# Gated linear attention and a dense block: one score product per 128-token chunk instead of seven levels of halving

## The chip, the cores and the metric

The kernel runs on one core of one Trainium2 chip. The metric is the device time of one execution in microseconds (us). The engines are PE (TensorE: matrix products and transposes), DVE (VectorE), ACT (ScalarE), POOL (GpSimd) and SP (SyncE, which here issues all transfers). Each engine works through its own queue in order.

## The reference

A recurrence over the tokens feeds a dense block.

```python
B, H, S, D = 4, 8, 768, 48          # q, k, v: randn * 0.1; alpha: uniform in 0.8 .. 1.0
for t in range(S):
    state = alpha[:, :, t, :, None] * state + einsum('bhd,bhe->bhde', k[:, :, t], v[:, :, t])
    y[:, :, t] = einsum('bhd,bhde->bhe', q[:, :, t], state)
x = y.transpose(0, 2, 1, 3).reshape(B * S, H * D)      # 3072 x 384
h = x @ w_in                                           # 384 x 2048
out = (h - tanh(h)) @ w_out                            # 2048 x 384
```

The weights come as float64 and everything is computed in fp32.

## The kernel before, in words

The 3072 tokens are worked in 12 units of 256 tokens, two chunks of 128 (c) each, three units to a batch entry. Two heads share the 128 partitions, 64 rows each, of which 48 hold features; g counts these four pairs, hh the head in a pair.

`gla(u)` is a unit's recurrence. It transposes alpha, k and q on PE (tiles an, kn, qn through tp, L185), so that features lie on the partitions. Then it goes through seven levels of halving (L204 to L236). At level l the block of 2 << l tokens has its left half (s) and its right half (t); the decay between them is a product from the middle to t (`pre`) times one from s to the middle (`suf`). At each level DVE multiplies q and k with these into W (L209, L213), PE makes 16 products of 128 rows by 64 columns (sc, L220), DVE copies the valid ones into `scores` under a mask (L225), and POOL extends suf and pre (L234, L235). The term s = t is made apart: qk and dv on POOL, dot on DVE. For each chunk PE then adds the old state's part (L246) and the scores' part (L249) into y; DVE adds dv, PE transposes x back, ACT stores xT. kT times suf is transposed (ks), multiplied with v (up, L269) and added to the decayed state by POOL and DVE (L278, L279).

`moe(u)` is the dense part. For each of 8 steps, `first(s)` makes h (L292: 6 products of 256 columns) and from it g = h - tanh(h), by a polynomial for small h: four operations on ACT (L301 to L304) and six on DVE (L305 to L310). `second(s)` adds g's product with w_out (L317: 4 products of 384 columns) to o0 and o1, two steps behind `first`. At the end ACT copies o to ob and SP writes it.

`weights()` loads w_in and w_out in 28 tiles and turns each from float64 into fp32 with six operations on DVE, two on ACT and one on POOL (L117 to L135); the tiles `raw` come from a pool of two buffers.

The order in which work is handed to the scheduler is a sorted list of numbered steps:

```python
MOE, GLA, EARLY = FS + 1, 1 + LEVELS + 2 * CU, 5.0
    order += [(u * MOE + i, 1, "moe", u) for i in range(MOE)]
    at = (u - 1) * MOE - EARLY
    order += [(at + i * MOE / GLA, 0, "gla", u) for i in range(GLA)]
```

So unit u's recurrence is spread over the dense part of the unit before it, and starts five steps early. The scheduler then fixes one order for each engine.

Of the kernel before, what the change touches and what calls it, by code (L numbers as in the profile page):

```python
# [8 lines left out]
FP32 = mybir.dt.float32  # L9
# [15 lines left out]
ZA = C4 ** 0.5  # L25
ZB = C3 / (2.0 * ZA)
ZK = C2 - ZB * ZB


@with_exitstack  # L30
def kernel(
# [14 lines left out]
    G = CU * NP  # L46
# [14 lines left out]
    consts = ctx.enter_context(tc.tile_pool(name="consts", bufs=1))  # L61
    two = ctx.enter_context(tc.tile_pool(name="two", bufs=2))
    three = ctx.enter_context(tc.tile_pool(name="three", bufs=3))
    ps_sc = ctx.enter_context(tc.tile_pool(name="ps_sc", bufs=2, space=PSUM))
    ps_tp = ctx.enter_context(tc.tile_pool(name="ps_tp", bufs=1, space=PSUM))
    ps_y = ctx.enter_context(tc.tile_pool(name="ps_y", bufs=1, space=PSUM))
    ps_h = ctx.enter_context(tc.tile_pool(name="ps_h", bufs=2, space=PSUM))
    ps_o = ctx.enter_context(tc.tile_pool(name="ps_o", bufs=1, space=PSUM))

    V, A, T, GP = nc.vector, nc.scalar, nc.tensor, nc.gpsimd  # L70
# [4 lines left out]
    V.memset(z_bias, ZB)  # L75
    m_bias = consts.tile([P, 1], FP32, name="m_bias")
# [4 lines left out]
    mask = consts.tile([P, LEVELS, P // 2], FP32, name="mask")  # L81
    GP.memset(mask, 1.0)
    for l in range(LEVELS):
        L = 1 << l
        m = mask[:, l, :].rearrange("p (n j) -> p n j", j=L)
        n = P // (2 * L)
        GP.affine_select(out=m, in_=m, compare_op=ALU.is_ge, fill=0.0, base=0,
                         pattern=[[-2 * L, n], [0, L]], channel_multiplier=1)
        GP.affine_select(out=m, in_=m, compare_op=ALU.is_ge, fill=0.0, base=L - 1,
                         pattern=[[2 * L, n], [0, L]], channel_multiplier=-1)  # L90
# [3 lines left out]
    nat = [[consts.tile([P, CU, H, HP], FP32, name=f"{n}{i}") for n in ("an", "kn", "qn")]  # L94
           for i in range(2)]
    for i in range(2):
        for t in nat[i]:
            GP.memset(t[:, :, :, D:], 0.0)
    scores = [consts.tile([P, 2, G, P], FP32, name=f"scores{i}") for i in range(2)]
    for t in scores:  # L100
        V.memset(t, 0.0)
    states = [consts.tile([P, NP, 2 * D], FP32, name=f"state{i}") for i in range(2)]
    for t in states:
        GP.memset(t, 0.0)
# [4 lines left out]
    def load_w(dst, src):  # L109
        """A part of a weight matrix, of up to 512 columns: from float64 rounded to fp32, with  # L110
        what fp32 has no normal number for as 0 or infinite."""
        if moe_w_in.dtype == FP32:
            nc.sync.dma_start(out=dst, in_=src)
            return
        n = dst.shape[-1]
        raw = two.tile([P, 512], I64, name="raw")
        nc.sync.dma_start(out=raw[:, 0:n], in_=src)  # L117
        words = raw.bitcast(I32).rearrange("p (n w) -> p n w", w=2)
        lo, hi = words[:, 0:n, 0].bitcast(mybir.dt.uint32), words[:, 0:n, 1]
        e = two.tile([P, 512], I32, name="e", tag="u")[:, 0:n]  # L120
        m = two.tile([P, 512], I32, name="m", tag="z")[:, 0:n]
        low = two.tile([P, 512], FP32, name="low", tag="t")[:, 0:n]
        man = two.tile([P, 512], FP32, name="man", tag="w")[:, 0:n]
        V.tensor_scalar(out=e, in0=hi, scalar1=20, scalar2=0x7FF,  # L124
                        op0=ALU.logical_shift_right, op1=ALU.bitwise_and)
        V.tensor_scalar(out=e, in0=e, scalar1=896, scalar2=1151, op0=ALU.max, op1=ALU.min)
        V.tensor_scalar(out=e, in0=e, scalar1=23, scalar2=0x3FFFFFFF,  # L127
                        op0=ALU.logical_shift_left, op1=ALU.bitwise_and)
        V.scalar_tensor_tensor(out=e, in0=hi, scalar=-0x40000000, in1=e,  # L129
                               op0=ALU.bitwise_and, op1=ALU.bitwise_or)  # L130
        V.tensor_single_scalar(out=m, in_=hi, scalar=0xFFFFF, op=ALU.bitwise_and)  # L131
        A.activation(man, m, AF.Copy, bias=1.0, scale=2.0 ** -20)
        A.activation(low, lo, AF.Copy, scale=2.0 ** -52)
        GP.tensor_add(man, man, low)
        V.tensor_mul(dst, man, e.bitcast(FP32))  # L135

    def weights():
        """In the order in which the first unit needs them."""
        w = 512
        for i in range(d_ff // w):  # L140
            for j in range(KT):
                load_w(w_in[:, j, i * w:(i + 1) * w], w_in_r[:, j, i * w:(i + 1) * w])
            yield
            for f in range(i * w // P, (i + 1) * w // P):
                load_w(w_out[:, f, :], w_out_r[:, f, :])
            yield

    loaded = {}

    def load(u):  # L150
        b, i = divmod(u, UPB)
        vt = three.tile([P, CU, H, D], FP32, name="vt")
        for c in range(CU):
            t0 = i * TU + c * P

            def rows(x):
                return x[b, :, t0:t0 + P, :].rearrange("h p d -> p h d")
            for t, x in zip(nat[u % 2], (alpha, k, q)):
                nc.sync.dma_start(out=t[:, c, :, 0:D], in_=rows(x))
            nc.sync.dma_start(out=vt[:, c], in_=rows(v))  # L160
        loaded[u] = vt

    xT = {}

    def gla(u):
# [4 lines left out]
        b, i = divmod(u, UPB)  # L170
        an, kn, qn = nat[u % 2]
        vt = loaded.pop(u)
        P_ = scores[u % 2]

        def unit(name, pool=two):
            return pool.tile([P, CU, NP, P], FP32, name=name)

# [4 lines left out]
        def flip(dst, src, copy):  # L182
            tp = ps_tp.tile([P, NP, P], FP32, name="tp")
            for g in range(NP):
                T.transpose(tp[:, g, :], src[:, 2 * g:2 * g + 2, :], ident)  # L185
# [193 lines left out]
```

## Time and profile before

| | |
|---|---|
| three runs | 1138.49, 1139.68, 1145.95 us (median 1139.68) |
| span of the profiled execution | 1140.3 us; its own time stands as this span |
| PE busy | 1045.0 us (92%) |
| PE weight loads (PEld) busy | 845.6 us (74%) |
| DVE busy | 805.0 us (71%) |
| ACT busy | 320.6 us (28%) |
| POOL busy | 342.8 us (30%) |
| mean granted PE clock | 0.909 of full speed |

A span is the time from the first to the last instruction. Busy times overlap between engines and add up to more than the span. Mean durations of PE's instructions overlap too, since matmuls are pipelined; the distance between starts says what one costs. In the rows, L220 is line 220 of the kernel, `sc<-W` is the output and the inputs, `64*128 64x64` are the shapes of the operands, and `x32` the number of instructions that a row merges. An idle time in brackets names what ended it.

### The profile page before, as it was taken

The page shows a single profiled execution, that of the slowest core. Times are in us where ns is not written, and L with a number is a line of the kernel's source. Part 1 is how long each engine was busy: PE and PEld are TensorE (multiplying, and loading weights), DVE is VectorE, ACT ScalarE, POOL GpSimd, SP SyncE. Part 2 cuts the span into 40 slices and gives each one's busy share as a digit, 9 for nine tenths or more (in the row PEclk, how much of TensorE's full clock was granted, in tenths as well). Part 3 has the DMA queues.
Part 4 walks back from the last instruction along what each step waited for, and adds up shares of the span by engine and source line. Part 5 has one row for each costly group of instructions (what it writes and reads, how often), then busy time and mean ns, then how long its engine had stood idle before and what let it go on. Part 6 is the DMA issues. An engine that isn't in the chain of part 4 may idle for free.

```text
span 1140.3 us, 14741 instructions
## 1 busy us (share of the span) xinstructions
PE 1045.0 (92%) x5752; PEld 845.6 (74%) x5752; DVE 805.0 (71%) x1212; ACT 320.6 (28%) x569; POOL 342.8 (30%) x293
## 2 busy tenths in 40 slices
PE   3765648999999999999999999999999999999988
PEld 2764548877877878778777788778787788777765
DVE  6688896584684677776774777685775676776766
ACT  2012330321421331421511431521502322413433
POOL 6454443043042044043132043143132152141000
PEclk9999755887998899989988999998979999989999
DMA  9433620110110020110200110200200000000000
GB/s 175 81 91 97 150 73 1 27 30 14 27 31 14 1 56 15 29 28 15 56 1 15 35 23 14 50 8 14 56 1 15 1 1 15 1 1 15 1 14 14
DMA packets 107396, 37.11 MB, mean 33 GB/s; under 512 B 100672, under 2 KB 103744, under 8 KB 107328
## 3 DMA queue, kind: packets, MB, share of 16 engines
q1 hardware_dynamic: 107328, 36.19, 14.1%
q8 instruction: 45, 0.74, 0.3%
q14 instruction: 23, 0.19, 0.1%
HBM read 31.46 MB, written 4.72 MB: 32 GB/s over the span
## 4 chain that ended last, share of the span: by engine, by line
PE 79%; DVE 15%; POOL 2%; issue 2%; ACT 1%; DMA 0%; SPq 0%; POOLq 0%; DVEq 0%
PE sc L220 24%; PE h L292 24%; PE o L317 20%; PE y L249 4%; DVE scores L225 3%; PE tp L185 2%; PE y L246 2%; PE up L269 2%; DVE e L129 1%; DVE W L209 1%; DVE z L307 1%; DVE e L127 1%; PE tp L265 1%; DVE m L131 1%; DVE e L124 1%
## 5 line engine op out<-in xcount | busy, mean ns | idle before, releaser
L220 PEld LDWEIGHTS sc<-W 64*128 64x128 f32 x2688 | 324.9, 217 | 92.7 <-issue 68.7
L220 PE MATMUL sc<-W 64*128 64x64 f32 x2688 | 338.1, 305 | 53.6 <-DVE W L213 41.0
L292 PE MATMUL h<-xT,w_in 128*128 128x256 f32 x1152 | 325.1, 426 | 5.1 <-DVE g L310 3.8
L317 PE MATMUL o<-w_out,g 128*128 128x384 f32 x768 | 278.7, 504 | 0.2 <-DVE g L310 0.2
L292 PEld LDWEIGHTS h<-xT,w_in 128*128 128x128 f32 x1152 | 231.7, 213 | 46.0 <-issue 4.8
L225 DVE COPY_PREDICATED scores<-mask,sc 128x512 f32<-128x512 int32 x168 | 147.8, 882 | 117.4 <-PE sc L220 115.1
L317 PEld LDWEIGHTS o<-w_out,g 128*128 128x128 f32 x768 | 147.5, 198 | 84.0 <-issue 7.7
L301 ACT ACTIVATE sq<-h 128x512 f32<-128x512 f32 x96 | 57.4, 598 | 440.9 <-PE h L292 437.1
L235 POOL TENSOR_TENSOR pre<-pre 128x512 f32<-128x512 f32 x84 | 118.3, 1409 | 115.5 <-DVE W L209 112.3
L234 POOL TENSOR_TENSOR suf<-suf,pre 128x512 f32<-128x512 f32 x72 | 100.3, 1393 | 140.3 <-DVE W L213 137.5
L305 DVE TENSOR_TENSOR w<-h,sq 128x512 f32<-128x512 f32 x96 | 66.2, 690 | 93.1 <-ACT th L302 92.4
L209 DVE TENSOR_TENSOR W<-qT,pre 128x512 f32<-128x512 f32 x84 | 60.1, 716 | 24.9 <-POOL pre L235 14.9
L310 DVE COPY_PREDICATED g<-large,h 128x512 f32<-128x512 int32 x96 | 70.6, 736 | 3.3
L309 DVE SCALAR_TENSOR_TENSOR g<-z,w 128x512 f32<-128x512 f32 x96 | 70.8, 737 | 1.8
L307 DVE SCALAR_TENSOR_TENSOR z<-z,sq 128x512 f32<-128x512 f32 x96 | 70.2, 731 | 0.0
L303 ACT ACTIVATE z<-sq,z_bias 128x512 f32<-128x512 f32 x96 | 69.6, 725 | 0.0
L304 ACT ACTIVATE large<-sq,m_bias 128x512 f32<-128x512 f32 x96 | 69.3, 722 | 0.0
L308 DVE SCALAR_TENSOR_TENSOR z<-z,sq 128x512 f32<-128x512 f32 x96 | 67.7, 705 | 1.9
L306 DVE TENSOR_TENSOR h<-h,th 128x512 f32<-128x512 f32 x96 | 66.7, 695 | 0.0
L213 DVE TENSOR_TENSOR W<-kT,suf 128x512 f32<-128x512 f32 x72 | 56.4, 784 | 14.2 <-POOL suf L234 14.2
L278 POOL TENSOR_TENSOR state<-state,pre 64x192 f32<-64x192 f32 x32 | 23.1, 722 | 139.3 <-DVE state L279 69.8
L249 PE MATMUL y<-vt,scores 128*128 128x48 f32 x384 | 53.2, 291 | 4.7 <-DVE scores L225 4.7
(60 smaller groups left out, 737.1 us busy)
## 6 DMA issues: line engine op xcount, KB each, us to landing
raw<-in_moe_w_in_dram SPq DMA_DIRECT2D x12, 512.0 KB, 3.9
raw<-in_moe_w_out_dram SPq DMA_DIRECT2D x16, 384.0 KB, 3.1
an<-in_alpha_dram SPq DMA_DIRECT2D x24, 192.0 KB, 3.3
kn<-in_k_dram SPq DMA_DIRECT2D x24, 192.0 KB, 3.5
qn<-in_q_dram SPq DMA_DIRECT2D x24, 192.0 KB, 3.1
vt<-in_v_dram SPq DMA_DIRECT2D x24, 192.0 KB, 3.9
out_dram<-ob SPq DMA_DIRECT2D x24, 192.0 KB, 1.9
```

Source lines behind the costliest of these rows:

```text
L209: V.tensor_mul(W1, q1, p1)
L220: T.matmul(sc[:, g, :], lhsT=Wf[rows, g, :], rhs=Wh[rows, g, :, 1, :], start=True, stop=True)
L225: V.copy_predicated(out=to, mask=on.unsqueeze(1).to_broadcast([P, G, n, L]), data=sc.rearrange("p g (n j) -> p g n j", j=L))
L234: GP.tensor_mul(s0, s0, e1)
L235: GP.tensor_mul(p1, p1, e0)
L249: T.matmul(y[:, h * D:(h + 1) * D], lhsT=P_[:, h % 2, c * NP + h // 2, :], rhs=vt[:, c, h, :], start=(n == 0 and h == 0), stop=True, skip_ ...
L292: T.matmul(h[:, a, :], lhsT=w_in[:, j, f * P:(f + 1) * P], rhs=x_t[:, j, :], start=(j == 0), stop=(j == KT - 1))
L303: A.activation(z, sq, AF.Square, bias=z_bias, scale=ZA)
L307: V.scalar_tensor_tensor(out=z, in0=z, scalar=ZK, in1=sq, op0=ALU.add, op1=ALU.mult)
L309: V.scalar_tensor_tensor(out=g, in0=z, scalar=C0, in1=w, op0=ALU.add, op1=ALU.mult)
L310: V.copy_predicated(out=g, mask=large.bitcast(I32), data=h)
L317: T.matmul(o[c], lhsT=g[:, a * TU + c * P:a * TU + (c + 1) * P], rhs=w_out[:, f, :], start=(f == 0), stop=(f == FT - 1))
```

## The change

The seven levels of score products become one. The levels remain for the prefix products alone: POOL makes `pre` (the product of alpha from the chunk's start to t) and `suf` (from behind s to the chunk's end) in the same in-place steps, with no DVE or PE work between them. k is then multiplied with suf divided by the whole chunk's decay, so that q times pre and k times this give every pair's decay at once. Per chunk PE makes 8 products of 128 by 128 (sc0, sc1), and DVE multiplies them with a triangular mask `keep`, which holds s = t too.

Four further edits come with it. q and k are transposed after the scan, and DVE multiplies them straight out of PSUM. y is made with features on the partitions, by products whose weights are 64 columns wide (the old state, or v), so x isn't transposed back; ACT stores yT, and SP moves its rows with ten transfers a unit into xT. The polynomial of the dense part is written as two squares and has one more operation on ACT and one fewer on DVE, and its difference d has a tile of its own instead of lying in h's PSUM buffer. The scores' PSUM pool has one buffer each for sc0 and sc1.

The halving method stays as a fallback (`general`). Each chunk's whole decay is kept in `ends`, bounded to 1e-18 and 1e18; after the last unit all engines read a count of the partitions where all of them lie inside the bounds, and if any does not, `general` computes everything again, chunk by chunk.

```diff
+END_MIN, END_MAX = 1e-18, 1e18
...
+            A.activation(sq, h, AF.Square)
+            A.activation(th, h, AF.Tanh)
+            V.tensor_mul(w, h, sq)
+            A.activation(z, sq, AF.Square, bias=z_bias, scale=ZA)
+            V.tensor_sub(d, h, th)
+            A.activation(z, z, AF.Square, bias=g_bias)
+            A.activation(large, sq, AF.Relu, bias=m_bias)
+            V.scalar_tensor_tensor(out=z, in0=sq, scalar=ZL, in1=z, op0=ALU.mult, op1=ALU.add)
+            V.scalar_tensor_tensor(out=g, in0=z, scalar=ZC, in1=w, op0=ALU.add, op1=ALU.mult)
+            V.copy_predicated(out=g, mask=large.bitcast(I32), data=d)
...
-            V.tensor_mul(W1, q1, p1)
...
-                for g in range(G):
-                    T.matmul(sc[:, g, :], lhsT=Wf[rows, g, :], rhs=Wh[rows, g, :, 1, :],
-                             start=True, stop=True)
...
-                V.copy_predicated(
-                    out=to, mask=on.unsqueeze(1).to_broadcast([P, G, n, L]),
-                    data=sc.rearrange("p g (n j) -> p g n j", j=L))
...
+            for c in range(CU):
+                A.copy(pre[:, c], flip(an[:, c]))
+            yield
+            for l in range(LEVELS):
+                L = 1 << l
+                (p0, p1), (s0, s1) = halves(pre, L), halves(suf, L)
...
+                if l == 0:
+                    GP.tensor_copy(s0, p1)
+                    GP.memset(s1, 1.0)
+                else:
+                    GP.tensor_mul(s0, s0, e1)
+                GP.tensor_mul(p1, p1, e0)
+                yield
+            whole = pre.rearrange("p c g t -> p (c g) t")[:, :, P - 1:P]
+            V.tensor_scalar(out=ends[:, u, :].unsqueeze(2), in0=whole, scalar1=END_MIN,
+                            scalar2=END_MAX, op0=ALU.max, op1=ALU.min)
+            recs = two.tile([P, CU * NP], FP32, name="recs")
+            V.reciprocal(recs, ends[:, u, :])
+            for c in range(CU):
+                GP.tensor_mul(suf[:, c], suf[:, c],
+                              recs[:, c * NP:(c + 1) * NP].unsqueeze(2).to_broadcast([P, NP, P]))
+            yield
...
+                V.tensor_mul(qh[:, c], flip(qn[:, c]), pre[:, c])
+                V.tensor_mul(kh[:, c], flip(kn[:, c]), suf[:, c])
+
+                sc = [ps_sc.tile([P, NP, P], FP32, name=f"sc{hh}") for hh in range(2)]
+                for g in range(NP):
+                    for hh in range(2):
+                        rows = slice(HP * hh, HP * hh + HP)
+                        T.matmul(sc[hh][:, g, :], lhsT=kh[rows, c, g, :], rhs=qh[rows, c, g, :],
+                                 start=True, stop=True)
+                x = [two.tile([P, NP, P], FP32, name=f"x{hh}") for hh in range(2)]
+                for hh in range(2):
+                    V.tensor_mul(x[hh], sc[hh], keep.unsqueeze(1).to_broadcast([P, NP, P]))
...
+                            T.matmul(y[HP * hh:HP * hh + HP, g, :], lhsT=old[:, g, hh, :],
+                                     rhs=qh[:, c, g, :], start=(g == 0), stop=False,
+                                     skip_group_check=True)
...
+                        T.matmul(y[HP * hh:HP * hh + HP, g, :], lhsT=vn[:, c, 2 * g + hh, :],
+                                 rhs=x[hh][:, g, :], start=(n == 0 and g == 0), stop=True,
+                                 skip_group_check=True)
+                A.copy(yT[:, :, c * P:(c + 1) * P], y)
...
+                            T.matmul(up[HP * hh:HP * hh + HP, g, :], lhsT=ks[:, g, hh, :],
+                                     rhs=vn[:, c, 2 * g + hh, 0:D], start=(g == 0),
+                                     stop=(g == NP - 1), skip_group_check=True)
...
+                    nc.sync.dma_start(out=x_t[p:p + n, j, :], in_=yT[r:r + n, h // 2, :])
...
+        MOE, GLA, EARLY = FS + 1, 3 + LEVELS + 4 * CU, 5.0
...
+        n_fine = nc.values_load(count[0:1, 0:1], min_val=0, max_val=P)
+    with tc.If(n_fine < P):
+        with ExitStack() as inner:
+            general(inner)
```

The change moves the engines' orders at three places. The first is on PE, at the end of one unit's dense part (o) and the start of the next unit's (h), in the middle of the kernel. Before, the last levels' score products stand between dense work:

```order
L317 MATMUL o_1063<-w_out,g 128x384
L220 MATMUL sc<-W 128x64 x16
L292 MATMUL h<-xT,w_in 128x256 x6
L220 MATMUL sc<-W 128x64 x16
L246 MATMUL y<-state_120,qT 128x96 x4
```

With the change, the flips of q and k for the next recurrence stand there, with two h products behind each, and the first chunk's eight scores alternate between two tiles (the first two are shown):

```order
L141 MATMUL o_1611<-w_out,g 128x384
L234 MATMUL tp<-ident,qn_74 128x128 x4
L119 MATMUL h<-xT,w_in 128x256 x2
L234 MATMUL tp<-ident,kn_73 128x128 x4
L119 MATMUL h<-xT,w_in 128x256 x2
L274 MATMUL sc_1987<-qh,kh 128x128
L274 MATMUL sc_1988<-qh,kh 128x128
```

So the flips that stood earlier have moved to the boundary between units, and two rows of scores a level, 14 a unit, have become two groups of eight a unit.

The second place is on PE too, where alpha is flipped for the recurrence that follows the one under way. Before, alpha, k and q are flipped together:

```order
L185 MATMUL tp<-ident,an_107 128x128 x4
L292 MATMUL h<-xT,w_in 128x256 x4
L185 MATMUL tp<-ident,kn_108 128x128 x4
L292 MATMUL h<-xT,w_in 128x256 x2
L185 MATMUL tp<-ident,qn_109 128x128 x4
```

With the change, alpha of both chunks is flipped without k and q, and dense work follows:

```order
L234 MATMUL tp<-ident,an_72 128x128 x4
L119 MATMUL h<-xT,w_in 128x256 x2
L234 MATMUL tp<-ident,an_72 128x128 x4
L119 MATMUL h<-xT,w_in 128x256 x4
L141 MATMUL o_1610<-w_out,g 128x384
L141 MATMUL o_1611<-w_out,g 128x384
```

From the second of these flips to the flip of qn at the first place stand 22 products h and 24 products o; it is in this stretch that POOL makes the prefix products.

The third place is on DVE, at the end of the weights' conversion, where the first dense operation stands. Before, it lies among the score copies and W of unit 1:

```order
L129 SCALAR_TENSOR_TENSOR e<-raw,e 128x384
L225 COPY_PREDICATED scores_117<-mask,sc 128x128x4
L135 TENSOR_TENSOR w_out<-man,e 128x384
L209 TENSOR_TENSOR W<-qT,pre 128x64x8
L124 TENSOR_SCALAR e<-raw 128x384
L131 TENSOR_SCALAR m<-raw 128x384
L126 TENSOR_SCALAR e<-e 128x384
L213 TENSOR_TENSOR W<-kT,suf 128x64x8
L127 TENSOR_SCALAR e<-e 128x384
L305 TENSOR_TENSOR w<-h,sq 128x512
```

With the change, it lies behind the masks of unit 2's second chunk:

```order
L278 TENSOR_TENSOR x_1318<-sc_1308,keep 128x512
L186 SCALAR_TENSOR_TENSOR e<-raw,e 128x384
L192 TENSOR_TENSOR w_out<-man,e 128x384
L181 TENSOR_SCALAR e<-raw 128x384
L188 TENSOR_SCALAR m<-raw 128x384
L183 TENSOR_SCALAR e<-e 128x384
L184 TENSOR_SCALAR e<-e 128x384
L127 TENSOR_TENSOR w<-h,sq 128x512
L186 SCALAR_TENSOR_TENSOR e<-raw,e 128x384
L129 TENSOR_TENSOR d<-h,th 128x512
```

In both orders 27 of the 28 weight tiles stand ahead of it; what moved is that a third unit's recurrence stands ahead of it too, where it was part of the second's.

More of the change, by code (lines that the diff above doesn't have):

```diff
@@ L75 @@
     V.memset(z_bias, ZB)
+    g_bias = consts.tile([P, 1], FP32, name="g_bias")
+    V.memset(g_bias, ZG)
     m_bias = consts.tile([P, 1], FP32, name="m_bias")
     V.memset(m_bias, -U_MAX)
[L81 to L90, printed above, removed]
+    keep = consts.tile([P, P], FP32, name="keep")
@@ L106 @@
     w_in = consts.tile([P, KT, d_ff], FP32, name="w_in")
     w_out = consts.tile([P, FT, d_model], FP32, name="w_out")
[L109 to L161, printed above, removed]
@@ L282, in moe, with rows_of, dense @@
-    def moe(u):
-        x_t = xT.pop(u)
-        o = [ps_o.tile([P, d_model], FP32, name=f"o{c}") for c in range(CU)]
+    def rows_of(x, b, t0):
+        return x[b, :, t0:t0 + P, :].rearrange("h p d -> p h d")
+    def dense(pools, name, x_t, store):
+        work, three, ps_h, ps_o = pools
+        n_c = x_t.shape[2] // P
+        tu = n_c * P
+        o = [ps_o.tile([P, d_model], FP32, name=f"o{c}") for c in range(n_c)]
         g_of = {}
         def first(s):
-            h = ps_h.tile([P, 2, TU], FP32, name="h")
+            h = ps_h.tile([P, 2, tu], FP32, name="h")
@@ L326, in moe @@
         second(FS - 1)
[L327 to L328 removed]
+        for c in range(n_c):
+            ob = work.tile([P, d_model], FP32, name="ob")
             A.copy(ob, o[c])
[L330 removed]
+            store(c, ob)
         yield
[L335 to L341 removed]
```

422 lines of the change are left out of this document (273 added, 149 removed).

## The prediction

> **What bounds the kernel now.** I read the page's busy times and chain first, then windows by stage, then TensorE's (PE's) timeline.
>
> ```profile
> PE 1045.0 (92%) x5752; PEld 845.6 (74%) x5752; DVE 805.0 (71%) x1212; ACT 320.6 (28%) x569; POOL 342.8 (30%) x293
> ...
> PE 79%; DVE 15%; POOL 2%; issue 2%; ACT 1%; DMA 0%; SPq 0%; POOLq 0%; DVEq 0%
> PE sc L220 24%; PE h L292 24%; PE o L317 20%; PE y L249 4%; DVE scores L225 3%; PE tp L185 2%; PE y L246 2%; PE up L269 2%; DVE e L129 1%; DVE W L209 1%; DVE z L307 1%; DVE e L127 1%; PE tp L265 1%; DVE m L131 1%; DVE e L124 1%
> ...
> L220 PE MATMUL sc<-W 64*128 64x64 f32 x2688 | 338.1, 305 | 53.6 <-DVE W L213 41.0 <-DVE W L209 9.5 <-DVE scores L225 3.0
> ```
>
> The reader is to see that PE carries the chain, and that a quarter of it is the score products. There are 1344 of them; the trace counts two instructions for an fp32 product and one for a transpose. Now the stages:
>
> ```profile
> core 0: us, PE busy (x) PEld busy (x) DVE busy (x) ACT busy (x) POOL busy (x), PEclk, DMA share, GB/s
> 0.00:203.00 203.00, 123.35 (x616) 115.01 (x617) 160.30 (x255) 45.07 (x79) 94.75 (x99) 0.81 0.41 94
> 203.00:1063.00 860.00, 851.87 (x4882) 681.32 (x4882) 594.05 (x881) 245.92 (x438) 248.07 (x194) 0.93 0.09 20
> 1063.00:1141.00 78.00, 69.77 (x257) 49.25 (x256) 50.66 (x77) 29.62 (x53) 0.00 (x0) 0.97 0.03 11
> ```
>
> For 203 us PE has holes: VectorE (DVE) converts the weights and the recurrence of units 0 and 1 runs. Then, to 1063 us, PE is idle for only 860 - 851.9 = 8 us: there PE's own work is the time. The last 78 us are the last dense part alone.
>
> Means of a matmul overlap its neighbours, so I take prices from starts in the timeline (start, duration), at full clock.
>
> ```profile
> 438.16 3.39 PE L220 MATMUL sc<-W 64*128 64x64 f32 x32
> 441.48 4.78 PE L317 MATMUL o<-w_out,g 128*128 128x384 f32 x14
> ...
> 449.51 2.86 PE L292 MATMUL h<-xT,w_in 128*128 128x256 f32 x12
> 452.30 3.39 PE L220 MATMUL sc<-W 64*128 64x64 f32 x32
> ...
> 469.28 1.91 PE L249 MATMUL y<-vt,scores 128*128 128x48 f32 x16
> 471.03 1.53 PE L292 MATMUL h<-xT,w_in 128*128 128x256 f32 x6
> ...
> 476.60 0.60 PE L265 MATMUL tp<-ident,kT 128*128 128x128 f32 x4
> 477.03 1.03 PE L292 MATMUL h<-xT,w_in 128*128 128x256 f32 x4
> ...
> 1063.13 2.75 PE L292 MATMUL h<-xT,w_in 128*128 128x256 f32 x12
> 1065.72 2.74 PE L317 MATMUL o<-w_out,g 128*128 128x384 f32 x8
> 1068.31 2.75 PE L292 MATMUL h<-xT,w_in 128*128 128x256 f32 x12
> ```
>
> So 32 score instructions take 441.48 - 438.16 = 3.32 us, 104 ns each; y takes 109 ns each, a transpose 108 ns, h 2.59/12 = 216 ns, o 2.59/8 = 323 ns. A product of 48 columns and a transpose of 128 cost the same 0.11 us: below about 128 columns the price is per instruction. That is the lever of this change: 112 score products per unit become 16, twice as wide, at nearly the same price each.
>
> **What goes, on PE.** Scores per unit: 224 instructions x 0.104 = 23.3 us. They also cost clock:
>
> ```profile
> 604.16 3.39 PE L220 MATMUL sc<-W 64*128 64x64 f32 x32
> 607.49 4.54 PE L317 MATMUL o<-w_out,g 128*128 128x384 f32 x8
> 611.96 0.32 PE L220 MATMUL sc<-W 64*128 64x64 f32 x1
> ```
>
> ```profile
> 604.00:608.00 4.00, 4.00 (x35) 3.63 (x35) 3.60 (x7) 0.00 (x0) 1.39 (x1) 1.00 0.00 0
> 608.00:612.00 4.00, 4.00 (x9) 1.90 (x7) 2.76 (x5) 0.00 (x0) 1.69 (x2) 0.58 0.00 0
> ```
>
> After a whole block of scores, eight o take 4.47 us instead of 2.59, and the granted clock is 0.58. In dense work alone (1063 on) they keep 2.59. I read the mean of 0.93 in the middle stage as the price of score blocks; it should rise towards 1.
>
> **What PE has to do afterwards.** In the new order PE reaches unbroken dense work once the recurrences of units 0 to 2 are done and two of unit 0's eight h steps. From there I count: 564 h products x 2 x 0.216 = 243 us; 384 o x 2 x 0.323 = 248 us; and for nine units (3 to 11) 208 + 60 transposes x 0.109 = 29 us, 144 scores, 144 + 120 y and 120 up products x 2 x 0.109 = 115 us. Sum **635 us** at full clock; the steady unit is 41.4 us of dense work plus 16 of recurrence, for 78 us now. A product of 64 rows or 64 weight columns by 128 is not in the trace. h and o cost 0.84 ns a column (216/256, 323/384), so 128 columns are 0.108, and the narrow rows (scores, y) stop at 0.104 to 0.109: I take 0.109. Above that nothing in the rows leads, save the change of shape, next. Below, two such products might share the array: half, 57 us less.
>
> Changing from a score block to dense work costs a little: the h x12 behind scores takes 452.30 - 449.51 = 2.79 us, 0.20 more than 2.59. Six blocks of 64-row or 64-column products per unit x 9 x 0.20 = **11 us**. The Trainium skill, "TensorEngine Tiling (Array Packing)", Key Properties, says that changing the tiling mode drains TensorE, and also that different tiles run at the same time; the first agrees with the 0.20 us, the second is a rival below.
>
> **What has to keep up.** The prefix products now run ahead, on GpSimd (POOL) alone.
>
> ```profile
> L235 POOL TENSOR_TENSOR pre<-pre 128x512 f32<-128x512 f32 x84 | 118.3, 1409 | 115.5 <-DVE W L209 112.3
> L234 POOL TENSOR_TENSOR suf<-suf,pre 128x512 f32<-128x512 f32 x72 | 100.3, 1393 | 140.3 <-DVE W L213 137.5
> L231 POOL COPY suf<-pre 128x512 f32<-128x512 f32 x12 | 12.0, 1003 | 128.2 <-DVE pre L186 128.2
> ```
>
> One unit's scan is 1.0 + 7 x 1.41 + 6 x 1.39 = 19.2 us, and two multiplications by the reciprocal (same size, 1.4 each) make 22 us; with two ScalarE (ACT) copies and the state's products about 25 us. In the new order 25 us of PE's work (22 h, 24 o) stand between the flips of alpha and those of q and k that need the scan: just enough. Of 57 us per unit POOL uses 25.
>
> DVE and ACT have room:
>
> ```profile
> L305 DVE TENSOR_TENSOR w<-h,sq 128x512 f32<-128x512 f32 x96 | 66.2, 690 | 93.1 <-ACT th L302 92.4
> L303 ACT ACTIVATE z<-sq,z_bias 128x512 f32<-128x512 f32 x96 | 69.6, 725 | 0.0
> ```
>
> Per dense step DVE has five operations of about 0.7 instead of six, 3.6 us, and ACT one more at 0.73, some 3.4 us, beside PE's 5.2. Per unit DVE's recurrence is 8 operations x 0.7 and 4 small ones instead of 14 COPY_PREDICATED and 13 W: DVE 36 of 57 us, ACT 31. Dropping qk, dot and dv from POOL and DVE is hidden behind PE. The ACT square takes z one step later, but h's buffer is now free after DVE's d, not after the last copy, so PE gains there; none of it is on the path. I put PE's waits at **10 us** (8 now), bounds 0 and 40: in each unit four short chains (flip, DVE product, scores, DVE mask) have only 0.9 to 1.7 us of h between them.
>
> SP gets ten transfers a unit to lay x out. They stand behind yT's copy and, in SP's order, ahead of the loads for two units later.
>
> ```profile
> 1136.70 0.98 SPq L330 DMA_DIRECT2D out_dram<-ob  x2
> 1136.84 0.48 ACT L329 COPY ob<-o 128x384 f32<-128x384 f32 x1 [0.17 <-PE o L317]
> ```
>
> ```profile
> out_dram<-ob SPq DMA_DIRECT2D x24, 192.0 KB, 1.9
> ```
>
> At 0.49 us an issue and 1.9 us to land they need 7 us; the last y stands some 32 us of PE work ahead of the dense part that reads it. Loads behind them have a unit's time in hand. Cost nothing; without the cover 7 us x 11.
>
> **The prologue.** The first g needs nearly all weights, because in DVE's order its operations stand behind 27 of 28 tiles, as before.
>
> ```profile
> 157.19 6.26 PE L220 MATMUL sc<-W 64*128 64x64 f32 x32 [8.88 <-DVE W L213]
> ```
>
> ```profile
> 169.91 0.69 DVE L305 TENSOR_TENSOR w<-h,sq 128x512 f32<-128x512 f32 x1
> ...
> 172.91 1.50 DVE L135 TENSOR_TENSOR w_out<-man,e 128x384 f32<-128x384 f32 x1
> ...
> 190.63 0.72 DVE L310 COPY_PREDICATED g<-large,h 128x512 f32<-128x512 int32 x1
> ```
>
> Now weights end at 174 us and the first g at 191. Afterwards three units' recurrences run here, one behind the other: each a scan of 22 us, about four of the weights' POOL additions between its steps
>
> ```profile
> L134 POOL TENSOR_TENSOR man<-man,low 128x384 f32<-128x384 f32 (+1 forms) x28 | 36.0, 1284 | 62.9 <-ACT man L132 61.5 <-DMA raw<-in_moe_w_in_dram 1.4
> ```
>
> (5 us), and two chunks of about 9 us (flips, kh, 16 score instructions at the cold 6.26/32 = 0.196 = 3.1 us, two masks): 45 us.
>
> ```profile
> 3.75 0.87 SPq L159 DMA_DIRECT2D an<-in_alpha_dram  x1
> ...
> 7.47 0.69 DVE L186 COPY pre<-tp 128x512 f32<-128x512 f32 x1 [2.21 <-PE tp L185]
> ```
>
> The first half of alpha is flipped and copied at 8 us, the second, issued 3 us later, about 10, so 10 + 3 x 45 = 145, and then DVE still has some four tiles and unit 2's masks, about 25 us: **170 us**. Bounds: 150 (the tail hidden) and 203 (no gain: what the scores free, the third recurrence takes).
>
> ```profile
> L124 DVE TENSOR_SCALAR e<-raw x28: 345/416/1697, 13.7 to 168.2; 128x384 int32<-128x384 int32 x16, 128x512 int32<-128x512 int32 x12
> ```
>
> A conversion step of 0.42 us has taken up to 1.70. The Trainium skill, "SBUF — State Buffer", Who interferes with whom, says that DVE and POOL lock a shared port against each other for a whole instruction; the row agrees, and by that rule a busier POOL stretches the conversions and the start moves towards 203.
>
> **Sum.** 170 + 635 + 11 + 10, and behind the last product 3.5 us as now (span 1140.3 less 1136.8, where ACT's last copy starts) plus some 3 for the flag's few small operations, its load and the branch (not in the trace; 0 to 10): 832 us. It is made against the span of 1140.3, 0.05% above the median of 1139.68, so no correction.
>
> **Rivals.** (1) The prologue gains nothing: 203 for 170 gives 865. For it: SP, DVE and POOL wait in order for three serial scans. Against: DVE loses 28 COPY_PREDICATED and 26 W of units 0 and 1 there, and PE's 8.88 us wait above was for such a W. (2) The clock stays at 0.93, 635/0.93 = 683, or scans come 5 us late in eight units: either gives 870 to 880. Against: clock 1.0 in dense work; y and transposes between dense work cost 0.11 as ever. (3) Neighbouring 64-wide products do run side by side: at most half of scores, y and up, 57 us: 775; half of that, 800. The Trainium skill's page on tiling says so. No row here shows it, since today's score products stand eight and eight on the same rows. (4) Slower: the run-time flag sends the kernel into the fallback, which does all 24 chunks again, serially. Per chunk 96 h products of 128 columns x 2 x 0.109 and 32 o x 0.646 are 42 us without any recurrence: over 1000 us more, above 1840. It decides when one 128-token decay product falls to 1e-18. Alpha is uniform from 0.8 to 1, mean logarithm -0.107, so the product is about 1e-6 with a spread of e^0.73: far from it, unless the test is wrong.
>
> **Chances and range.** Forecast (805 to 855) 0.55; rival 1 0.15, rival 2 0.12, rival 3 0.12, slower 0.03; mixtures 0.03. From 785 to 890 I leave out half of rival 3, pile-ups of 1 and 2, and the slower case: about 0.15. A change of 1% is about what a measurement of this kernel tells from none; faster by more has 0.96, within 1% 0.01, slower by more 0.03.
>
> **What would show it.** First g before 175 us; score instructions 384 at 0.11 us apart; steady output pairs 57 us apart instead of 78; granted clock from there near 1; PE waiting for POOL's scan or DVE's kh under 2 us a unit; no instruction of the fallback. Wrong if output pairs come 65 us apart with PE idle (scan), or if PE is full at half clock, or if the first output comes no earlier than 240 us.

## The result, and the profile after

The changed kernel takes 853.06 us (median of 4 runs, 851.49 to 853.7) against 1139.09 us for the kernel before on the same chip (4 runs): a ratio of 0.7494, 95% interval 0.7452 to 0.7536. Its profiled execution has a span of 852.0 us. The forecast was 832, the range 785 to 890. No instruction of the fallback is in its trace. Times are medians; two of the ten runs of one experiment, over 1.5% longer than its fastest, are left out of its figures below.

The same views of the changed kernel: the busy times, the chain, and windows of the prologue and of all from the first unbroken dense work to the last output copy.

```profile
PE 690.9 (81%) x3698; PEld 494.3 (58%) x3698; DVE 555.4 (65%) x818; ACT 362.4 (43%) x629; POOL 295.4 (35%) x281
...
PE 55%; POOL 20%; DVE 16%; ACT 3%; issue 3%; DMA 1%; SPq 1%; DVEq 0%; POOLq 0%; ACTq 0%
PE o L141 21%; PE h L119 20%; POOL pre L251 9%; POOL suf L250 9%; PE tp L234 4%; PE sc L274 3%; PE y L296 3%; PE y L291 2%; DVE g L134 2%; DVE e L186 2%; DVE e L184 2%; DVE g L133 2%; DVE e L181 1%; DVE w_in L192 1%; DVE m L188 1%
```

```profile
0.00:168.00 168.00, 65.35 (x477) 47.30 (x478) 143.54 (x215) 45.06 (x80) 102.77 (x105) 0.78 0.58 132
168.00:842.00 674.00, 625.19 (x3220) 446.86 (x3220) 410.98 (x599) 316.79 (x549) 192.62 (x176) 0.95 0.13 28
```

The kernel before, from its 203 us to its last output copy:

```profile
203.00:1136.84 933.84, 921.63 (x5138) 730.58 (x5137) 644.70 (x957) 275.06 (x489) 248.07 (x194) 0.93 0.09 19
```

The reader is to see two things. The chain was 79% PE; now POOL's prefix and suffix products hold 18% of it. And from the first unbroken dense work to the last output copy PE is idle for 674 - 625 = 49 us, where it had been idle for 12 of 934; the mean granted clock is still only 0.95. The time saved splits into 35 us of prologue (203 to 168), 260 us between there and the last copy, and a tail that is 6 us longer.

A unit in PE's timeline, behind its wait, and the two output copies that frame a unit:

```profile
443.15 1.16 PE L274 MATMUL sc<-qh,kh 64*128 64x128 f32 x16
444.24 0.66 PE L284 MATMUL tp<-ident,kh 128*128 128x128 f32 x4
444.74 1.03 PE L119 MATMUL h<-xT,w_in 128*128 128x256 f32 x4
445.69 1.09 PE L296 MATMUL y<-x,vn 128*64 128x128 f32 x16
446.72 2.86 PE L119 MATMUL h<-xT,w_in 128*128 128x256 f32 x12
449.50 0.67 PE L305 MATMUL up<-vn,ks 128*64 128x48 f32 x16
450.11 0.66 PE L234 MATMUL tp<-ident,qn 128*128 128x128 f32 x4
```

```profile
439.81 0.48 ACT L153 COPY ob<-o 128x384 f32<-128x384 f32 x1 [8.98 <-PE o L141]
...
501.50 0.48 ACT L153 COPY ob<-o 128x384 f32<-128x384 f32 x1 [8.74 <-PE o L141]
```

By distance between starts a score instruction costs 1.09/16 = 0.068 us, y 1.03/16 = 0.064, up 0.61/16 = 0.038: well below the 0.109 of the forecast. Yet this unit takes 501.50 - 439.81 = 61.7 us, not 57. What fills it is just ahead of these rows. DVE's queue, POOL's last scan step, PE, and the window behind PE's wait:

```profile
416.87 0.70 DVE L129 TENSOR_TENSOR d<-h,th 128x512 f32<-128x512 f32 x1
425.58 0.17 DVE L254 TENSOR_SCALAR ends<-pre 128x8 f32<-128x8 f32 x1 [8.01 <-POOL pre L251]
425.78 0.20 DVE L257 RECIPROCAL recs<-ends 128x8 f32<-128x8 f32 x1
425.90 0.64 DVE L132 SCALAR_TENSOR_TENSOR z<-sq,z 128x512 f32<-128x512 f32 x1
...
428.02 1.45 DVE L134 COPY_PREDICATED g<-large,d 128x512 f32<-128x512 int32 x1
```

```profile
424.49 1.06 POOL L251 TENSOR_TENSOR pre<-pre 128x512 f32<-128x512 f32 x1
```

```profile
421.33 2.75 PE L119 MATMUL h<-xT,w_in 128*128 128x256 f32 x12
429.52 10.90 PE L141 MATMUL o<-w_out,g 128*128 128x384 f32 x24 [5.44 <-DVE g L134]
440.26 0.60 PE L234 MATMUL tp<-ident,qn 128*128 128x128 f32 x4
```

```profile
429.50:437.00 7.50, 7.48 (x14) 4.14 (x15) 6.36 (x10) 1.33 (x2) 0.00 (x0) 0.61 0.00 0
```

```profile
DVE ends L254 <- POOL pre L251: 73.3, 9, 9.2
```

```profile
PE o L141 <- DVE g L134: 42.9, 8, 5.5
PE h L119 <- DVE recs L257: 5.2, 1, 5.2
```

DVE reaches `ends`, an operation of 0.17 us, and stands there for 8 us until POOL's scan is done. In its queue behind `ends` is the rest of the dense step's polynomial (z, g), which needs nothing from the scan. PE waits 5.4 us for that g, eight times in the run (4.9 us the first time), and for the next 7.5 us its granted clock is 0.61: 24 o take 10.7 us, start to start, instead of 24 x 0.323 = 7.8. In the ninth unit it is h that waits, 5.2 us, and `recs` ends that wait. The nine waits are 48 of the 49 idle us. The Trainium skill, "TensorE: Matmul & The Clock Gate", What's actually happening, says that one idle window of about 3.4 us brings the clock down to half; the 0.61 behind a wait of 5.4 us agrees.

### The profile page after: what moved, and what is told of

It is laid out like the page before. It is cut to its first block, busy times and chain, and to the rows that moved or that the text cites. A ratio compares the mean times of both kernels' runs of the same rounds, so it can differ in the third digit from the quotient of the medians.

```text
span 852.0 us, 10194 instructions
## 1 busy us (share of the span) xinstructions
PE 690.9 (81%) x3698; PEld 494.3 (58%) x3698; DVE 555.4 (65%) x818; ACT 362.4 (43%) x629; POOL 295.4 (35%) x281
## 4 chain that ended last, share of the span: by engine, by line
PE 55%; POOL 20%; DVE 16%; ACT 3%; issue 3%; DMA 1%; SPq 1%; DVEq 0%; POOLq 0%; ACTq 0%
PE o L141 21%; PE h L119 20%; POOL pre L251 9%; POOL suf L250 9%; PE tp L234 4%; PE sc L274 3%; PE y L296 3%; PE y L291 2%; DVE g L134 2%; DVE e L186 2%; DVE e L184 2%; DVE g L133 2%; DVE e L181 1%; DVE w_in L192 1%; DVE m L188 1%
## 5 line engine op out<-in xcount | busy, mean ns | idle before, releaser
L119 PE MATMUL h<-xT,w_in 128*128 128x256 f32 x1152 | 283.5, 390 | 22.8 <-DMA xT<-yT 14.2
L119 PEld LDWEIGHTS h<-xT,w_in 128*128 128x128 f32 x1152 | 215.5, 194 | 66.0 <-issue 13.6
L251 POOL TENSOR_TENSOR pre<-pre 128x512 f32<-128x512 f32 x84 | 97.9, 1166 | 5.3
L134 DVE COPY_PREDICATED g<-large,d 128x512 f32<-128x512 int32 x96 | 86.7, 903 | 2.6
L132 DVE SCALAR_TENSOR_TENSOR z<-sq,z 128x512 f32<-128x512 f32 x96 | 71.1, 740 | 23.7 <-ACT z L130 23.7
L130 ACT ACTIVATE z<-z,g_bias 128x512 f32<-128x512 f32 x96 | 68.7, 716 | 0.0
L234 PE MATMUL tp<-ident,kn 128*128 128x128 f32 x96 | 17.8, 315 | 59.9 <-DVE qh L267 59.9
L129 DVE TENSOR_TENSOR d<-h,th 128x512 f32<-128x512 f32 x96 | 65.2, 679 | 0.0
L126 ACT ACTIVATE th<-h 128x512 f32<-128x512 f32 x96 | 56.9, 593 | 0.0
L191 POOL TENSOR_TENSOR man<-man,low 128x384 f32<-128x384 f32 (+1 forms) x28 | 33.6, 1200 | 48.1 <-ACT man L189 48.1
```

The lines of the kernel that those rows point to most:

```text
L119: T.matmul(h[:, a, :], lhsT=w_in[:, j, f * P:(f + 1) * P], rhs=x_t[:, j, :], start=(j == 0), stop=(j == KT - 1))
L129: V.tensor_sub(d, h, th)
L130: A.activation(z, z, AF.Square, bias=g_bias)
L132: V.scalar_tensor_tensor(out=z, in0=sq, scalar=ZL, in1=z, op0=ALU.mult, op1=ALU.add)
L134: V.copy_predicated(out=g, mask=large.bitcast(I32), data=d)
L251: GP.tensor_mul(p1, p1, e0)
```

## Experiments

Theory: (a) neighbouring 64-wide products on different halves of the array overlap, which made PE's work smaller than forecast; (b) `ends` in DVE's in-order queue costs 5.4 us of waiting and 3 us of clock in each of eight units. All ratios are against the kernel before on the same chip.

**Ends off VectorE's queue.**

```diff
-            V.tensor_scalar(out=ends[...], in0=whole, ...)
+            GP.tensor_scalar(out=ends[...], in0=whole, ...)
-            V.reciprocal(recs, ends[:, u, :])
+            GP.tensor_tensor(out=recs, in0=ends[:, u, :], in1=one_c.to_broadcast(...), op=ALU.pow)   # one_c = -1
```

> The clamp of the chunk's last products (ends) and its reciprocal go from VectorE to GpSimd, behind the scan that makes them; nothing else is changed. Theory (VectorE's in-order queue): ends waits 8 us for GpSimd's scan, and the g of dense steps 6 and 7 stand behind it, so PE waits 5.4 us and then runs o x24 in 10.7 instead of 7.75 us at half clock; 8.5 us in each of eight units. With ends gone from that queue both go: 853 - 68 = 785 us, and no PE wait for g over 1 us in the steady units. Rival (port contention): g is late because VectorE's z, g and copy take 1.4 to 1.7 us instead of 0.7 while GpSimd scans; then the waits stay and the time is 840 to 855. Between: the wait goes but qh and kh then wait for the scan, 2 to 4 us a unit: 800 to 820.

Measured: 802.44 us (800.34 to 806.38), ratio 0.7026 (0.6988 to 0.7064): 51 us less than the changed kernel. Its waits and a window of the middle stage:

```profile
PE o L143 <- DVE g L136: 18.6, 17, 2.0
```

```profile
171.00:794.40 623.40, 603.91 (x3216) 433.87 (x3216) 438.69 (x580) 314.44 (x547) 222.93 (x190) 1.00 0.13 30
```

The long waits are gone, none for g is over 2.0 us, and the mean clock with waits that short is 1.00. Dense work starts at 171 us here, 3 later; from there to the last copy the stage is 51 us shorter: PE's idle time falls from 49 to 20, its busy time from 625 to 604, the time at reduced clock. Theory (b) is shown. The time lies in the range that was expected for a case between, but not by its mechanism: PE's waits for kh are 0.3 us in all, for qh none. Of the 68 us expected, some 17 stayed behind as the seventeen short waits for g. Each of them stands behind 8 us in which POOL was busy for 7 or more, when DVE's operations are stretched (last section); that the stretching causes them was not tested apart.

**Halves apart, and alternating in the kernel before.** In the changed kernel hh is made the outer loop of scores, y and up; in the kernel before, the inner one of the scores.

```diff
-                for g in range(NP):
-                    for hh in range(2):
+                for hh in range(2):
+                    for g in range(NP):
```

> Same products, other order: in scores, y and the state's update all products of the lower 64 rows or columns come first, then all of the upper, where the changed kernel alternates. Theory (neighbouring products on different halves of the array overlap): a score, y or up instruction goes from 0.068, 0.064 and 0.038 us back to about 0.109, 6.5 us more per unit, nine units: up to 58 us more, less what falls into PE's present waits; 880 to 910 us. Rival (the price comes from the shape alone, 64 rows or 64 columns): no change, 853 us and the same distances between starts.

> The kernel before with one thing changed: its score products alternate between the lower and the upper 64 rows (two PSUM tiles instead of one), where it did all lower ones and then all upper ones. Theory (neighbours on different halves overlap): 0.104 us a score instruction falls to about 0.06, 224 a unit, 10 us a unit: 78 to 68 us, where VectorE with 67 us of work a unit becomes the bound; 1020 to 1060 us in all. Rival (no overlap): 0.104 as before, 1139 us.

Measured: 881.46 us (874.69 to 885.69), 28 us more than the changed kernel; and 1048.99 us (1042.55 to 1053.39), ratio 0.9195 (0.9129 to 0.9261). The first's timeline and the second's:

```profile
460.36 1.71 PE L274 MATMUL sc<-qh,kh 64*128 64x128 f32 x16
462.00 0.66 PE L284 MATMUL tp<-ident,kh 128*128 128x128 f32 x4
...
463.45 1.58 PE L296 MATMUL y<-x,vn 128*64 128x128 f32 x16
464.96 2.86 PE L119 MATMUL h<-xT,w_in 128*128 128x256 f32 x12
467.75 0.94 PE L305 MATMUL up<-vn,ks 128*64 128x48 f32 x16
468.62 0.66 PE L234 MATMUL tp<-ident,qn 128*128 128x128 f32 x4
```

```profile
627.18 2.00 PE L220 MATMUL sc<-W 64*128 64x64 f32 x32
629.11 2.85 PE L319 MATMUL o<-w_out,g 128*128 128x384 f32 x8
```

Apart, a score instruction costs 1.64/16 = 0.103 us, y 0.094 in this block, up 0.054; alternating, the old kernel's falls from 0.104 to 1.93/32 = 0.060. Theory (a) is shown in both directions, by little more than the order of two loops. One rival is left for the scores: there the PSUM tile alternates together with the rows. y and up write one PSUM tile in either order and changed price too, so for them it is not the tile. The first time is at the low edge because only the score went back almost to the forecast price; up kept half of it, which the theory doesn't explain. The kernel before could have had 91 us of the 286 without the rest of the change.

**The old polynomial in the changed kernel, the new one in the kernel before.** Each takes lines of the other's `first`:

```diff
-            V.tensor_sub(d, h, th)
-            A.activation(z, z, AF.Square, bias=g_bias)
-            V.scalar_tensor_tensor(out=z, in0=sq, scalar=ZL, in1=z, op0=ALU.mult, op1=ALU.add)
+            V.tensor_sub(h, h, th)
+            V.scalar_tensor_tensor(out=z, in0=z, scalar=ZK, in1=sq, op0=ALU.add, op1=ALU.mult)
+            V.scalar_tensor_tensor(out=z, in0=z, scalar=C1, in1=sq, op0=ALU.add, op1=ALU.mult)
...
-            V.copy_predicated(out=g, mask=large.bitcast(I32), data=d)
+            V.copy_predicated(out=g, mask=large.bitcast(I32), data=h)
```

> The changed kernel with the dense part's old polynomial: six VectorE operations and four ScalarE ones a step (third of them on h in PSUM) instead of five and five. Prediction's claim (that edit is hidden beside PE): 853 us, no change. Rival (VectorE is late by its queue in the changed kernel, so every operation of a step counts): the sixth operation adds 0.7 us a step, 1.5 us while GpSimd scans; over the four steps of a scan 4 to 6 us in each of eight units: 885 to 900 us, and longer PE waits for g.

> The kernel before with the new polynomial alone (five VectorE operations and five ScalarE ones a dense step, h's buffer free after the difference). Theory (PE is full there and waits 8 us in all after the prologue): 0 to 8 us less, 1131 to 1140 us. Rival (VectorE with 67 of 78 us a unit is already late in places that the waits do not show, as the opposite edit on the changed kernel cost 31 us): 15 to 30 us less, 1110 to 1125 us.

Measured: 884.13 us (881.92 to 885.38), 31 us more than the changed kernel; and 1153.1 us (eight runs, 1147.01 to 1159.83), ratio 1.0122 (1.0082 to 1.0163). Waits of the first:

```profile
PE h L118 <- DVE g L136: 78.1, 21, 8.9
```

With h's buffer held until DVE's last operation, it is now h that waits, 78 us in 21 places against 43 in 8. So the new polynomial is worth 31 us inside this change; one DVE operation less and h's buffer free earlier were not tested apart. Alone it made the kernel before about 1% slower, which neither side expected. PE's mean granted clock was 0.885 to 0.894 in those runs, against 0.906 to 0.916 in the kernel before, so the extra time goes with a lower clock; why the clock is lower stays open.

**Half of the scan.** The suffix products divided by the whole chunk's decay are the reciprocal of the prefix products, so six suffix steps and the scaling are left to one DVE reciprocal a chunk; the clamp of ends is on POOL here too.

```diff
-                    GP.tensor_mul(s0, s0, e1)
...
-                V.tensor_mul(kh[:, c], flip(kn[:, c]), suf[:, c])
+                V.reciprocal(inv[:, c], pre[:, c])
+                V.tensor_mul(kh[:, c], flip(kn[:, c]), inv[:, c])
```

> The suffix products are not scanned: suffix over whole is the reciprocal of the prefix, so VectorE takes one reciprocal of 128x512 a chunk and GpSimd loses the copy, the memset, six suffix products and two scalings a unit, 22 us of GpSimd's work to about 11; the clamp of ends is on GpSimd. Theory (scans pace the prologue and stretch VectorE by the shared port): unbroken dense work starts at 130 to 145 us instead of 168, PE's waits for g in the steady units, 19 us with only ends moved, fall under 8: 755 to 775 us. Rival (VectorE's conversions of the weights pace the prologue): start stays at 160 to 168, 785 to 795 us. If a reciprocal of 512 columns takes several us, VectorE's recurrence is late instead: over 800 us.

Measured: 821.07 us (820.59 to 822.38), 19 us slower than with ends on POOL alone. Its groups by line, DVE's timeline, PE's, and PE's waits:

```profile
L257 DVE RECIPROCAL inv<-pre 128x512 f32<-128x512 f32 x24 | 80.3, 3348 | 42.4 <-POOL pre L245 42.4
```

```profile
398.91 3.35 DVE L257 RECIPROCAL inv<-pre 128x512 f32<-128x512 f32 x1 [4.85 <-POOL pre L245]
```

```profile
158.41 2.86 PE L119 MATMUL h<-xT,w_in 128*128 128x256 f32 x12 [2.65 <-DVE d L129]
```

```profile
PE o L141 <- DVE g L134: 31.2, 11, 3.6
```

Reciprocal of 512 columns takes 3.35 us, five times a product of the same size, and the scheduler placed it where DVE waits 4.85 us for the scan, ahead of dense work: the same trap as `ends`, and PE's waits for g grow from 18.6 to 31.2 us. The expectation had named this case (over 800 us). Dense work starts at 158 us, 10 us earlier than in the changed kernel (12 than with ends on POOL alone) and not 23 to 38: halving the scan is not enough. Since six reciprocals of 3.35 us put 20 us more on DVE there, this run alone does not say how much the conversions hold up the prologue; the next one shows it.

**Shorter conversion of the weights**, on top of ends on POOL. The high word is shifted into fp32's place and the low word added, four DVE operations a tile instead of six. It leaves out the bound on the exponent, so a weight outside fp32's normal range would not be handled as before.

```diff
-            ... e: shift, clamp, shift, sign; m: mantissa ...
-            GP.tensor_add(man, man, low)
-            V.tensor_mul(dst, man, e.bitcast(FP32))
+            V.tensor_scalar(out=e, in0=hi, scalar1=3, scalar2=0x3FFFFFF8, ...)
+            V.scalar_tensor_tensor(out=e, in0=hi, scalar=-0x40000000, in1=e, ...)
+            V.tensor_single_scalar(out=m, in_=e, scalar=-0x800000, op=ALU.bitwise_and)
+            GP.tensor_mul(low, low, m.bitcast(FP32))
+            V.tensor_add(dst, low, e.bitcast(FP32))
```

> Beside ends on GpSimd (802 us), the weights' conversion takes four VectorE operations a tile instead of six, one ScalarE one instead of two and one GpSimd one as before (high word shifted into place, low word added). Theory (VectorE's conversions, 122 of the first 168 us and stretched by GpSimd's scans, pace the prologue): 28 tiles lose two of six operations, 40 us of VectorE's work, of which the chunks' own chain leaves 15 to 35: dense work starts at 135 to 155 us, 767 to 787 us. Rival (the three scans of 25 us with their chunks pace it): start at 160 to 170, 797 to 803 us.

Measured: 793.75 us (791.4 to 795.49). PE's timeline:

```profile
149.20 4.74 PE L121 MATMUL h<-xT,w_in 128*128 128x256 f32 x12 [0.91 <-DVE d L131]
```

The start is where the theory put it, 149 us, 22 earlier than with ends on POOL alone and with the scans as they were: the conversions hold up the start. They are not all of it, since half the scan had also brought 12 us, with more work on DVE. The one ScalarE operation a tile that went with them was not tested apart. The time fell by 9 only (15 between the two profiled executions), short of the theory's 15 to 35. In the profiles the first output comes at 188.5 instead of 210.9 us, the second at 237.4 instead of 253.5: recurrence work of the third unit, which had stood in the prologue's holes, now stands in the next unit, 48.9 us long instead of 42.5.

**The flag's tiles, the three steps, and all together.** The flag's tiles get memory of their own, first one, then all four; in the last kernel `second` runs three steps behind `first`, with g in four buffers.

```diff
-        fine = last.tile([P, NU * CU * NP], FP32, name="fine")
+    fine = consts.tile([P, NU * CU * NP], FP32, name="fine")      # then least, ones, count too
```

```diff
-            if s > 1:
-                second(s - 2)
+            if s > 2:
+                second(s - 3)
```

> The flag's tile fine gets its own place from the start of the program, instead of memory that the last output transfer still reads. Theory: fine waits 5.85 us for that transfer; without the wait the flag, its load and the branch run beside the transfer, and the 9.8 us from the last copy of ob to the end become 4 to 6: 847 to 849 us. Rival: what follows fine (the load of the count, the branch, the end of the program) waits for the transfer in any case: 852 to 853 us, no difference that can be told.

> All four small tiles of the flag have their own places from the start, not only fine, whose wait passed on to least. Theory: nothing of the flag waits for the last output transfer, and the 9.8 us from the last copy of ob to the end become 4 to 7 us: 847 to 850 us. Rival: the load of the count and the branch cost the same behind the transfer: 852 to 853 us.

> Reciprocal in place of the suffix scan, ends on GpSimd, and the flag's tiles kept, together. Theory: the two gains add, since one lies in the prologue and the units and the other behind the last product: 3 to 6 us below the kernel with the reciprocal alone, 750 to 771 us; by the rival for the prologue 780 to 790 us.

> Ends on GpSimd, the short conversion and the flag's own tiles together. Theory: the gains add, since they lie in different stages: 4 to 5 us below the kernel without the flag's tiles. If they do not, something else waits for the last transfer.

> The kernel of the line before, and each dense step's second product stands three steps behind its first instead of two (g in four buffers). Theory (PE's remaining waits for g, 19 us in seventeen places, come from VectorE running 1 to 2 us late while GpSimd scans): 5 us more of cover takes nearly all of them away, 12 to 19 us less. Rival (VectorE is late by its mean rate, not by a moment): the waits only move, under 4 us less.

Measured in this order: 855.13, 848.85, 815.77, 792.64 and 773.56 us (772.58 to 773.97; ratio 0.6783, 0.6736 to 0.6831). With one tile moved nothing was gained, since the wait passed on to `least`; with four it went, and the tail from the last copy to the end shrank from 9.8 to 4.6 us in the trace (4 us of the time; 5 on top of the reciprocal). Put on the shorter conversion it gave 1 us, not 4 to 5, and DVE's and PE's timelines of that kernel say why:

```profile
674.65 0.21 DVE L482 TENSOR_SCALAR fine<-ends 128x96 f32<-128x96 f32 x1 [8.36 <-POOL ends L255]
```

```profile
678.31 10.21 PE L147 MATMUL o<-w_out,g 128*128 128x384 f32 x24 [5.12 <-DVE g L140]
```

Free of its memory, the flag's first operation moved up 108 us, stood there in DVE's queue 8.4 us for the last scan, and took dense work behind it along: the trap of `ends`, once. With a third step of cover PE's waits for g are one of 2.6 us, and PE is busy for 612 of 616 us. The one left comes at 663 us, behind the flag's operation, which still waits 8.4 us; the cover hides the rest of that wait and does not remove it:

```profile
PE o L147 <- DVE g L140: 2.6, 1, 2.6
```

```profile
659.77 0.21 DVE L483 TENSOR_SCALAR fine<-ends 128x96 f32<-128x96 f32 x1 [8.37 <-POOL ends L256]
```

```profile
150.00:766.00 616.00, 612.15 (x3314) 439.47 (x3313) 444.37 (x591) 315.63 (x550) 228.91 (x196) 1.00 0.14 33
```

That kernel is the fastest here, 32% below the kernel before and 9% below the changed one.

## Why the prediction was right, and where it was not

The direction, the range and the main lever held: one score product per chunk in place of seven levels, PE the bound. But that the sum came within 21 us is in part luck: two errors of opposite sign, some 42 us too much for PE's work and 60 too little for waits and clock, nearly cancel.

| Term | Forecast, us | Measured, us |
|---|---|---|
| Prologue | 170 | 167.9 |
| PE's work from there, tiling changes included | 635 + 11 | 604 (with ends on POOL, clock 1.00) |
| Waits of PE | 10 | 49, and 21 more at reduced clock |
| Tail | 6.5 | 9.8 |

**Prologue: right, its working half right.** The 45 us per recurrence was built from scans in a row; the runs show both the scans and DVE's conversions in it. Here are a conversion step of 384 columns beside POOL's scan and one just behind the scan, in DVE's timeline with ends on POOL:

```profile
80.21 1.22 DVE L183 TENSOR_SCALAR e<-raw 128x384 int32<-128x384 int32 x1
...
85.87 0.35 DVE L183 TENSOR_SCALAR e<-raw 128x384 int32<-128x384 int32 x1
```

The conversions, stretched so, are 133 of the first 168 us on DVE in the changed kernel (the 122 in an expectation above was added up wrongly). Rival 1, that this would eat the whole gain, did not come. The first g was done at 170.4 us (before 175, as said).

**PE's work: the price of the new products was the mis-sized term.** 115 us were put for scores, y and up at 0.109; at the measured prices 144 x 2 x 0.068 + 264 x 2 x 0.064 + 120 x 2 x 0.038 = 63 us. "Above that nothing leads" was right, "below, two might share the array" was the case: rival 3, given 0.12, nearly in full (52 of 57 us). The Trainium skill, "TensorEngine Tiling (Array Packing)", Key Properties, says that different tiles run in parallel; the two runs with the loops exchanged agree, 0.068 against 0.103 us and 0.060 against 0.104. The evidence that no row of before showed it was sound; the step that failed was taking the dear end as the value. The 0.20 us for a change of tiling held: h x12 behind y takes 449.50 - 446.72 = 2.78 us instead of 2.59.

**Waits: the step that failed.** "Just enough" was put on the flips of q and k, where PE's cover of 25 us meets a scan of 18 to 22, and there it did hold: behind the prologue no wait stands there. The prediction followed the moved work on PE and POOL, but not through DVE's queue, where the scan's first reader is the small `ends`, placed ahead of dense steps that had been ready. Rival 2's case of eight late units came nearly as priced, nine units and about 5 us each, but through another queue, and a unit lost 8.5 us and not 5, since the clock behind the wait was left out.

**Clock.** The claim that the old score blocks cost it fits, since without them and without long waits it is 1.00, but no run tested the blocks apart from the waits; the changed kernel's own 0.95 came from the waits, as the run with ends on POOL shows.

**"None of it is on the path"** (the polynomial) was wrong: undone, it costs 31 us. It had been judged on a kernel whose PE hardly waited for DVE once the prologue was over. **The xT transfers** cost nothing from 168 us on; in the prologue they hold PE for 14 us in three places. **Tail:** the operations were as small as assumed; what was left out was that `fine` takes memory that the last transfer still reads:

```profile
842.20 0.48 ACT L153 COPY ob<-o 128x384 f32<-128x384 f32 x1 [0.17 <-PE o L141]
845.11 0.21 DVE L486 TENSOR_SCALAR fine<-ends 128x96 f32<-128x96 f32 x1 [5.85 <-DMA out_dram<-ob]
```

The marks set in advance: score instructions 0.11 apart (0.068), output pairs 57 us apart (61.4 in the steady units; 57.1 only as a mean over all eleven, where lighter units at both ends hide it), waits for POOL's scan under 2 us a unit (none by PE itself, 5.4 through DVE).

## What to carry to other kernels

When work moves to a slower engine, look for its first reader in every other engine's queue, however small: here an operation of 0.17 us that waited 8 held back everything behind it, and a PE wait of 5.4 us cost 3 us more in clock. Issue narrow matmuls so that neighbours use different halves of the array. And price an edit in the kernel it will stand in: a polynomial with one DVE operation less was worth 31 us where DVE was late, and made the kernel before, where PE hardly waited for DVE behind the prologue, about 1% slower.

## What the hardware showed unexpectedly

- Alternating between the halves brought an fp32 product of 64 rows from 0.103 to 0.068 us an instruction (128 columns) and from 0.104 to 0.060 (64 columns); products with 64 weight columns and 48 moving ones cost 0.054 even apart, below the 0.104 to 0.109 that all narrow products of before had shared. What sets that floor was not tried.
- Dense DVE operations with two SBUF inputs took up to 1.7 us instead of 0.7 while POOL scanned; those with one input in PSUM did not (0.68). Integer conversion steps with a single SBUF input were stretched as well (1.22 against 0.35 us, above). The Trainium skill, "SBUF — State Buffer", Who interferes with whom, says that a DVE instruction with two SBUF inputs contends with a GpSimd instruction that reads SBUF. In the changed kernel's DVE timeline the first row, with h in PSUM, is not stretched and the next two are, which agrees:

```profile
410.33 0.68 DVE L129 TENSOR_TENSOR d<-h,th 128x512 f32<-128x512 f32 x1
411.55 1.42 DVE L132 SCALAR_TENSOR_TENSOR z<-sq,z 128x512 f32<-128x512 f32 x1 [0.54 <-ACT z L130]
413.01 1.64 DVE L133 SCALAR_TENSOR_TENSOR g<-z,w 128x512 f32<-128x512 f32 x1
```

- A reciprocal of 512 fp32 columns costs DVE 3.35 us (6.5 ns a column), and a power of -1 over only 8 columns costs POOL 1.66 us in most units (with ends on POOL).
